# A long convolution by FFT ahead of a wave MLP: the setup written in another order, with the inverse's e tables made in the first inverse

## The chip, the cores and the metric

The kernel runs on one core of a Trainium2 chip. The metric is device time in microseconds (us) of one execution. The time before is the median of three runs, 2074.11 us (2072.76 to 2074.3). Besides, one execution was recorded by the hardware profiler, and all durations below come from it. Engines are called PE (matrix products; PEld is its weight load), DVE (VectorE), ACT (ScalarE), POOL (GpSimd) and SP (SyncE, which only issues DMAs here).

## The reference, cut to what matters

```python
# x (8, 5696, 128), h (5696, 128), all float32
L = 2 * S                                    # 11392
Yf = np.fft.rfft(x, n=L, axis=1) * np.fft.rfft(h, n=L, axis=0)[None]
x = np.fft.irfft(Yf, n=L, axis=1)[:, :S, :]  # the long convolution
theta = x @ w_theta
y = einsum('ts,bsd->btd', w_tok_r, x * cos(theta)) \
  + einsum('ts,bsd->btd', w_tok_i, x * sin(theta))
u = x + y
out = u + maximum(u @ w_ch, 0)
```

The change touches only the convolution, and of it the tables, h's transform and the first of eight groups of x.

## The kernel before, in words

**The transform.** The length 11392 is N1 x N2 = 178 x 64. Of the 178 frequencies of the first direction, K1 = 90 are kept (the rest follow by symmetry), and the sequence fills NB = 89 rows. A forward transform has two stages. *Stage A* (`stage_a`, L229) multiplies the 89 rows of the data by the table `f1_t` (L238): 16 chunks of four products, each chunk in one PSUM tile that ACT (L245) or DVE (L243) copies into the tile `a`, turned. With `both` set, chunks 1, 3, 6, 8, 11 and 13 go to DVE and ten to ACT. *f2* (`f2`, L248) multiplies `a` by the table `w_t2` (L256): 12 chunks, eleven with 32 products and the last with eight, then after the last chunk WARM = 12 products on table data whose results nobody reads (L262).

**h.** Two POOL DMAs bring h into `u_t` (L123). Four copies on DVE (`h_copy`, L289) turn it to f16 in `h16`, 16 of each half's 64 columns at a time. Its stage A follows, then f2; `h_chunk` (L307) evicts each chunk on ACT (L315) or DVE (L313) into a staging in the two halves of the tile `uv_t`, halves the first and the last frequency (L318), and issues two DMA stores on SP's queue (L320) to `hf_hbm`: 24 stores. They reorder the data, so each group reads it back from there.

**x.** There are eight groups, four pairs of batches by two halves of the channels. Each has a stage A and a *stage B* (`stage_b`, L356): f2's chunks are evicted by ACT to `xs` (L372), multiplied on DVE by the spectrum of h (`hs`, L374, the last chunk in two parts L379) and written to `uv_t`. The spectrum's chunks come back through SP's queue (L365) into four `hs` buffers, chunk c+4 loaded when chunk c has been multiplied. *Stage C* (`stage_c`, L385) is the first inverse step: 16 chunks of 16 products with the tables `r_u` and `r_v` (L395, L396), evicted with the sign table `sgn` into the tile `g` by DVE (L403) or, for four chunks, by two ACT operations (L400, L401). *Stage D* (`stage_d`, L406) is the last step, with the table `e_t` (L418), into the tile `yt`, which SP stores (L433). For each group g, stage C of g is woven with stage A of g+1 and the loads of group g+2; then stage B of g+1 is woven with stage D of g. The loads of x are pairs of POOL DMAs (L145), eight pairs a group; from group 2 on, each pair stands behind a small POOL copy that reads a piece of `g` (L143), so that it starts only once stage C has come so far. PSUM has four tiles for all these stages.

**The tables.** Each is a sine or cosine of a number of turns. POOL counts indices (iota, L170) and multiplies them by a column of the small tile `lane` (L178; `lane` is made in L156 to L161 by iotas and four POOL scalings). DVE takes the whole turns off (`within`, L184 and L185) and makes the absolute value (L192); ACT takes the sine (L189) and the cosine (L196). The tables are `f1_t`; `w_t2` in three parts (`w_angles` L216, then `w_rest` L222, which fills the other columns by two DVE operations, L225 and L227); `r_u`, `r_v` (`r_table`, L331); `sgn` (`s_table`, L350); and `e_t` in three parts (`e_table`, L342, 90x979 each). `signs` (L208) makes the column `sign` on DVE. `make_identity` (L57) makes a matrix on POOL that only the later part reads.

**What sets the order.** A scheduler orders the instructions of the rest, but from L151 to L462 (`ordered`) DVE, ACT and POOL keep the order in which the code is written. An instruction that waits there holds back all that is written behind it for its engine. The written order of before: h's loads, lane, the turns of f1 and w, loads of x group 0, the turns of r; then on DVE f1's angles, signs, w_angles(0), w_angles(1), w_rest(0), the first h copy, w_rest(1), and stage A of h with the other copies at chunks 1, 3 and 5, w_angles(2) at 6 and w_rest(2) at 12; then h's f2; then the turns of e and the loads of x group 1 on POOL; the two r tables, the s table and e table 0; stage A of x group 0 with e table 1 in its middle; stage B of group 0 with e table 2 in its middle.

**The rest.** After the eight groups the kernel multiplies the result by `w_theta`, takes sines and cosines (L479 to L501), and mixes the tokens with two 5696 x 5696 matrices (products L1097 and L1176, sums L1183, transposes of the weights L791), where most of the time lies.

Of the kernel before, what the change touches and what calls it, by code (L numbers as in the profile page):

```python
# [10 lines left out]
F32 = mybir.dt.float32  # L11
BF16 = mybir.dt.bfloat16
# [10 lines left out]
def kernel(  # L23
# [10 lines left out]
    nc = tc.nc  # L34
# [19 lines left out]

    const_pool = ctx.enter_context(tc.tile_pool(name="const", bufs=1))
    ident_bf = const_pool.tile([P, P], BF16)
    make_identity(nc, ident_bf)  # L57
    half_pi = const_pool.tile([P, 1], F32)
    nc.vector.memset(half_pi, HALF_PI)
    zero_b = const_pool.tile([P, 1], F32)  # L60
# [97 lines left out]
    nc.gpsimd.iota(lane[:, 1:2], pattern=[[0, 1]], base=0, channel_multiplier=1,  # L158
                   allow_small_or_imprecise_dtypes=True)
    for n, (col, per) in enumerate(((1, N1), (0, NF), (0, N2), (1, NF))):  # L160
        nc.gpsimd.tensor_scalar(lane[:, n + 2:n + 3], lane[:, col:col + 1], 1.0 / per, None, op0=mult)  # L161
    of_k1, of_n2, of_r, of_e = (lane[:, n:n + 1] for n in range(2, 6))

    def index(pattern, tag):

        n = 1
        for _, c in pattern:
            n *= c
        k = s1.tile([P, n], F32, tag=tag, name=tag)
        nc.gpsimd.iota(k, pattern=pattern, base=0, channel_multiplier=0, allow_small_or_imprecise_dtypes=True)  # L170
        return k

    def turns_of(k, base, of, m, tag=None):

        n = k.shape[1]
        t = (s1.tile([P, n], F32, tag=tag, name=tag) if tag else
             s2.tile([P, 11 * NB], F32, tag="turn", name="turn")[:, :n])[:m]
        nc.gpsimd.tensor_scalar(t, k[:m], float(base), of[:m], op0=add, op1=mult)  # L178
        return t
# [8 lines left out]
    def sine(out_, r, sign):  # L188
        nc.scalar.activation(out_, r, AF.Sin, bias=zero_b[:r.shape[0]], scale=-sign * TWO_PI)  # L189
# [6 lines left out]
        nc.scalar.activation(out_, k, AF.Sin, bias=half_pi[:k.shape[0]], scale=-TWO_PI)  # L196

    f1_t = fc.tile([P, 2 * K1], F16)
    t_f1 = turns_of(index([[1, K1]], "k_f1"), 0, of_k1, NB, "t_f1")
    H2 = N2 // 2  # L200
    k_w = index([[1, WK], [N1, H2]], "k_w")
    t_w = [turns_of(k_w, WK * c, of_n2, P) for c in range(3)]
    w_t2 = keep.tile([P, K1, 3 * N2], F16, tag="keep", name="w_t2")
    assert WB + BT + 3 * P * 2 <= K1 * 3 * N2
# [3 lines left out]
    def signs():  # L208
        t, k = s1.tile([P, 1], F32, tag="s_t", name="s_t"), s1.tile([P, 1], F32, tag="s_k", name="s_k")
        nc.vector.tensor_scalar(t, lane[:, 1:2], 0.5, None, op0=mult)  # L210
        nc.vector.tensor_scalar(k, t, MAGIC, None, op0=add)
        nc.vector.scalar_tensor_tensor(t, k, MAGIC, t, op0=ALU.subtract, op1=ALU.subtract)
        absolute(k, t)
        nc.vector.tensor_scalar(sign, k, -4.0, 1.0, op0=mult, op1=add)
# [11 lines left out]
        w_ = w_.rearrange("p k (c u n) -> p k c u n", c=3, u=2)  # L226
        nc.vector.tensor_scalar(w_[:, :, :, 1], w_[:, :, :, 0], sign, None, op0=mult)  # L227

    def stage_a(lhs, both=False):  # L229

        st = {}

        def chunk(q):
            if q == 0:
                st["a"] = fa.tile([P, 2 * K1, HD], F16, tag="a", name="a_")
            ps = psum()
            for i in range(4):
                nc.tensor.matmul(ps[:, i // 2, (i % 2) * 2 * K1:(i % 2 + 1) * 2 * K1], lhs(q + i), f1_t[:NB],  # L238
                                 start=True, stop=True)
            a_out = st["a"][:, :, q:q + 4].rearrange("p k (a q) -> p k a q", a=2)  # L240
            a_in = ps[:, :, :4 * K1].rearrange("p a (q k) -> p k a q", q=2)
            if both and q // 4 % 5 % 2:
                nc.vector.tensor_copy(a_out, a_in)  # L243
# [4 lines left out]
    def f2(a_st, c):  # L248

        c0, ck = CHK[c]  # L250
        ps = psum()
        for j in range(ck):
            for ri in range(2):
                for e in range(2):
                    rows = slice(64 * e, 64 * e + 64)
                    nc.tensor.matmul(ps[:, e, j * HD:(j + 1) * HD],  # L256
                                     w_t2[rows, c0 + j, N2 * (1 - ri):N2 * (3 - ri)],
                                     a_st["a"][rows, ri * K1 + c0 + j, :],
                                     start=(ri == 0), stop=(ri == 1))
        if c == NCK - 1:  # L260
            for n in range(WARM):
                nc.tensor.matmul(ps[:, n % 2, ck * HD:ck * HD + 384], w_t2[:, 2, :P],  # L262
                                 w_t2[:, 0:2, :].rearrange("p k n -> p (k n)"), start=True, stop=True)
        return ps[:, :, :ck * HD].rearrange("p e (k d) -> p e d k", k=ck)
# [8 lines left out]

    for f in load_x(0):
        f()
    nc.gpsimd.memset(uv_t[:, 2 * UVW:], 0.0)
    k_r = index([[0, 2], [1, N2]], "k_r")
    t_r = [turns_of(k_r, 0, of_r, P, f"t_r{n}") for n in range(2)]
    k_f = within(t_f1)
    absolute(k_f, t_f1)  # L280
    sine(f1_t[:NB, K1:], t_f1, -1)
    cosine(f1_t[:NB, :K1], k_f)
    signs()
    w_angles(0)
    w_angles(1)
    w_rest(0)

    def h_copy(d0):
        nc.vector.tensor_copy(h16[:NB, :, :, d0:d0 + 16],  # L289
                              u_t[:NB, :N2 * D].rearrange("p (n h d) -> p h n d", h=2, d=HD)[:, :, :, d0:d0 + 16])  # L290

    h_copy(0)
    w_rest(1)
    steps, a_h = stage_a(lambda q: h16[:NB].rearrange("p h n d -> p (h n) d")[:, :, q], True)
    for n, f in enumerate(steps):
        if n in (1, 3, 5):
            h_copy(8 * n + 8)
        if n == 6:
            w_angles(2)
        if n == 12:  # L300
            w_rest(2)
        f()

    hst = [t[:, :6 * D * CK].rearrange("p (c h d k) -> p c h d k", c=6, h=2, k=CK) for t in (u_t, v_t)]
    nc.gpsimd.memset(hst[(NCK - 1) // 6][:, (NCK - 1) % 6], 0.0)

    def h_chunk(c):  # L307
        c0, ck = CHK[c]
        ps = f2(a_h, c)
        h_ = hst[c // 6][:, c % 6]  # L310
        dst = h_[:, :, :, :ck]
        if c % 3 == 1:
            nc.vector.tensor_scalar(dst, ps, 16.0 / NF, None, op0=mult)  # L313
        else:
            nc.scalar.activation(dst, ps, AF.Copy, scale=16.0 / NF)  # L315
        for cc, j in ((0, 0), (NCK - 1, CHK[-1][1] - 1)):
            if c == cc:
                nc.vector.tensor_scalar(dst[:, :, :, j], dst[:, :, :, j], 0.5, None, op0=mult)  # L318
        for ri in range(2):
            nc.sync.dma_start(  # L320
                hf_hbm[:, c, :, ri, :].rearrange("h p n -> p h n"),
                h_[64 * ri:64 * ri + 64].rearrange("p h d k -> p h (d k)"))

    for c in range(NCK):
        h_chunk(c)
    r_u = fc.tile([P, P], F16)
    r_v = fc.tile([P, P], F16)
# [1 line left out]
    sgn = fc.tile([P, N2], F32)  # L329

    def r_table(n_, r_):  # L331
        t = t_r[n_]
        for q0 in range(2):
            for q1 in range(2):
                a_ = t[64 * q0:64 * q0 + 64, 64 * q1:64 * q1 + 64]
                nc.vector.tensor_scalar(a_, a_, 0.25 * (1 + n_ + q0 - q1), None, op0=add)
        k = within(t)
        sine(k, t, 1)
        nc.vector.tensor_scalar(r_[:, :N2 + EN], k[:, :N2 + EN], 0.125, None, op0=mult)
        nc.vector.tensor_scalar(r_[:, N2 + EN:], k[:, N2 + EN:], -0.125, None, op0=mult)  # L340

    def e_table(n):  # L342
        n0, t = 11 * n, t_e[n]
        k = within(t)
        absolute(k, t)
        t3, k3 = (z.rearrange("p (n m) -> p n m", m=NB) for z in (t, k))
        sine(e_t[:K1, n0:n0 + 11, 1, :], t3, -1)
        cosine(e_t[:K1, n0:n0 + 11, 0, :], k3)
# [89 lines left out]
    zz_n, ZB = [0], 3  # L438
    groups = [(bp, dh) for bp in range(B // 2) for dh in range(2)]

    def front(g, both=False):
# [4 lines left out]
        steps, a_st = stage_a(lambda q: x16[:NB, :, q], both)  # L446
        return (steps, *stage_b(a_st, dh))

    k_e = index([[1, 11], [N2, NB]], "k_e")
    t_e = [turns_of(k_e, 11 * n, of_e, K1) for n in range(3)]  # L450
    for f in load_x(1):
        f()
    r_table(0, r_u)
    r_table(1, r_v)
    s_table()
    e_table(0)
    a0, load0, b0 = front(0, True)
    for f in load0:
        f()
    woven(a0, [lambda: e_table(1)])  # L460
    woven(b0, [lambda: e_table(2)])
    ordered.close()  # L462
    setup.close()
    fg = pool("fft_g", 1, conv, side="right")
# [774 lines left out]
```

## Time and profile before

| what | value |
|---|---|
| median of three runs | 2074.11 us (2072.76 to 2074.3) |
| the profiled execution, its own time | 2068.87 us |
| its span in the trace | 2067.1 us |
| mean granted clock of PE over the span | 0.985 |
| busy share of the span: PE, DVE, POOL, ACT | 94%, 77%, 47%, 31% |
| first product on PE starts | 17.72 us |
| h's f2 starts | 32.49 us |
| stores of h's spectrum, first and last issue on SP | 35.41 and 54.78 us |
| first load of the spectrum issued | 55.44 us |
| first multiply of group 0 | 65.03 us |
| last multiply of group 0 | 85.0 us |
| last multiply of group 0 to first multiply of group 1 | 85.0 to 105.59 us |

The span runs from the first to the last instruction in the trace; the profiled execution's own time lies 1.77 us above it, and 5.24 us under the median of the runs. Starts are counted from the start of the span. The first 106 us hold all that the change touches; after it, from the second group on, one group follows the other every 37.5 to 40.4 us (first DVE eviction of stage C to the next group's), and the token mixing fills the rest.

### The profile page before, as it was taken

Reading aid. Unit: us, or ns where it says so; the run is one execution under the profiler, and the core shown is the slowest. Engines: PE = TensorE matmul, PEld = TensorE weight load, DVE = VectorE, ACT = ScalarE, POOL = GpSimd, SP = SyncE. Lnnn points to the kernel's source line nnn. Section 1 sums busy time; section 2 is a strip of 40 time slices with the busy share of each in tenths; the row PEclk is TensorE's granted clock in tenths of the full one; section 3 lists DMA queues with packets and bytes.
Section 4 is the critical chain, followed back from the end, with each engine's and each line's share of the span. In section 5 each row is a group of like instructions: output and inputs, shape, how many; then the busy total and the mean of one; then the engine's idle time right before and its main releaser. Section 6 shows DMA issues by size and latency. Waiting matters only on the chain.

```text
span 2067.1 us, 41585 instructions
## 1 busy us (share of the span) xinstructions
PE 1948.0 (94%) x15688; PEld 1080.5 (52%) x15865; DVE 1584.9 (77%) x2806; ACT 639.2 (31%) x971; POOL 964.7 (47%) x1764
## 2 busy tenths in 40 slices
PE   4788998889999999999999999999999999999998
PEld 3788888754444444444444444444444444444444
DVE  7787787877788888888877666877778677777767
ACT  4777777872323232333300000011111111111111
POOL 8232321266435363545475644454453535454450
PEclk9799999999999999999999999999999999999999
DMA  9799996999889898999999899788796979788793
GB/s 122 128 159 162 157 153 194 232 270 229 145 176 179 173 177 161 173 179 171 178 163 163 122 226 248 112 138 145 133 157 123 154 129 152 138 142 152 125 155 89
DMA packets 504489, 335.00 MB, mean 162 GB/s; under 512 B 184999, under 2 KB 457511, under 8 KB 503303
## 3 DMA queue, kind: packets, MB, share of 16 engines
q0 software_dynamic: 322208, 156.75, 59.7%
q1 hardware_dynamic: 176096, 164.05, 27.8%
q10 hardware_dynamic: 5984, 11.54, 1.6%
q8 instruction: 124, 2.03, 0.4%
q14 instruction: 77, 0.63, 0.1%
HBM read 377.11 MB, written 92.49 MB: 227 GB/s over the span
## 4 chain that ended last, share of the span: by engine, by line
PE 63%; DVE 5%; issue 2%; POOL 2%; DMA 1%; ACT 0%; DVEq 0%; POOLq 0%
PE m L1176 58%; PE m L1097 2%; DVE c L1183 2%; POOL ring L590 1%; DVE b L732 1%; PE v L878 1%; PE utp L871 1%; PE m L1180 1%; DMA ring<-in_moe_w_tok_i_dram 1%; DVE wt L791 1%; PE theta_ps L477 0%; PE tpz L819 0%; PE m L1063 0%; DMA ring<-in_moe_w_tok_r_dram 0%; POOL wl L838 0%
## 5 line engine op out<-in xcount | busy, mean ns | idle before, releaser
L590 POOL DMA_DIRECT2D ring<-in_moe_w_tok_i_dram x720 | 388.5, 545 | 659.9 <-DVE wt L791 579.0
L590 POOL DMA_DIRECT2D ring<-in_moe_w_tok_r_dram x720 | 387.2, 545 | 148.6 <-DVE wt L791 83.8
L791 DVE STREAM_TRANSPOSE wt<-ring 128x384 f32<-128x384 f32 (+2 forms) x720 | 360.0, 525 | 112.5 <-PE m L1176 69.3
L1176 PE MATMUL m<-b,wt 128*128 128x512 bf16 x1599 | 386.2, 380 | 4.1 <-DVE wt L791 1.7
L1176 PEld LDWEIGHTS <-wt 128*128 128x128 bf16 x1804 | 176.4, 98 | 219.8 <-DVE wt L791 7.5
L1183 DVE TENSOR_TENSOR c<-c,m 128x512 f32<-128x512 f32 x412 | 266.2, 672 | 0.4 <-PE m L1176 0.4
L873 ACT ACTIVATE ring<-utp 128x512 bf16<-128x512 bf16 x85 | 50.8, 597 | 582.5 <-PE utp L871 582.5
L395 PE MATMUL ps<-r_u,uv_t 128*128 128x128 f16 x1024 | 126.7, 220 | 9.0 <-DVE uv_t L379 5.9
L396 PE MATMUL ps<-r_v,uv_t 128*128 128x128 f16 x1024 | 125.8, 220 | 0.4
L374 DVE TENSOR_TENSOR uv_t<-xs,hs 128x2048 f16<-128x2048 f16 x88 | 105.9, 1225 | 25.6 <-ACT xs L372 15.5
L1097 PE MATMUL m<-b,wt 128*128 128x512 bf16 x466 | 111.2, 385 | 8.0 <-DMA b<-z_hbm 3.5
L868 ACT ACTIVATE ub<-c 128x512 bf16<-128x512 f32 x88 | 55.1, 629 | 191.0 <-DMA ring<-in_moe_w_tok_r_dram 112.4
L145 POOL DMA_DIRECT2D x<-in_x_dram x128 | 97.9, 770 | 34.9 <-PE ps L238 20.2
L395 PEld LDWEIGHTS <-uv_t 128*128 128x128 f16 x1024 | 100.6, 98 | 7.5 <-DVE uv_t L379 7.0
L396 PEld LDWEIGHTS <-uv_t 128*128 128x128 f16 x1024 | 100.5, 98 | 4.7 <-issue 3.0
L372 ACT ACTIVATE xs<-ps 128x1024 f16<-128x1024 f32 x96 | 91.4, 978 | 30.5 <-DVE uv_t L374 17.1
L1097 PEld LDWEIGHTS <-wt 128*128 128x128 bf16 x528 | 51.2, 99 | 67.0 <-issue 8.8
L256 PEld LDWEIGHTS <-w_t 64*128 64x128 f16 x3240 | 60.0, 101 | 27.1 <-issue 20.8
L479 ACT ACTIVATE red<-theta_ps,magic 128x512 f32<-128x512 f32 (+1 forms) x46 | 31.6, 688 | 135.6 <-PE theta_ps L477 109.6
L238 PE MATMUL ps<-f_t,x 89*128 89x180 f16 x512 | 59.7, 255 | 8.8 <-DVE a__784 L243 8.7
L821 ACT ACTIVATE ring<-tpz 128x512 bf16<-128x512 bf16 (+1 forms) x46 | 27.5, 597 | 130.8 <-PE tpz L819 114.9
L501 ACT ACTIVATE mag<-mag,half_pi 128x512 f32<-128x512 f32 (+1 forms) x90 | 65.1, 724 | 0.0
(2916 smaller groups left out, 3746.8 us busy)
## 6 DMA issues: line engine op xcount, KB each, us to landing
ring<-in_moe_w_tok_r_dram POOLq DMA_DIRECT2D x352, 96.0 KB, 4.5
ring<-in_moe_w_tok_i_dram POOLq DMA_DIRECT2D x352, 96.0 KB, 4.9
ring<-in_moe_w_tok_r_dram POOLq DMA_DIRECT2D x352, 80.0 KB, 4.5
ring<-in_moe_w_tok_i_dram POOLq DMA_DIRECT2D x352, 80.0 KB, 3.9
hs<-hf_hbm SPq DMA_DIRECT2D x192, 128.0 KB, 3.2
cp_hbm<-c SPq DMA_DIRECT2D x88, 256.0 KB, 2.5
c<-cp_hbm SPq DMA_DIRECT2D x88, 256.0 KB, 4.5
out_dram<-c SPq DMA_DIRECT2D x88, 256.0 KB, 4.3
```

The lines of the kernel that those rows point to most:

```text
L145: nc.gpsimd.dma_start(x16[p0:p1, e, n0:n0 + 16, :HD], bass.AP(tensor=src.tensor, offset=src.offset + (p0 * N2 + n0) * D + dh * HD, ap=[[N2 ...
L256: nc.tensor.matmul(ps[:, e, j * HD:(j + 1) * HD], w_t2[rows, c0 + j, N2 * (1 - ri):N2 * (3 - ri)], a_st["a"][rows, ri * K1 + c0 + j, :], s ...
L372: nc.scalar.activation(xs[:, :, :, :ck], ps, AF.Copy)
L374: nc.vector.tensor_tensor(uv[:, :, :, c0:c0 + ck], xs.rearrange("p e d k -> p e (d k)").unsqueeze(1).to_broadcast([P, 2, 2, HD * CK]), hv. ...
L395: nc.tensor.matmul(o, u_t[:, at:at + P], r_u, start=True, stop=False)
L396: nc.tensor.matmul(o, v_t[:, at:at + P], r_v, start=False, stop=True)
L501: nc.scalar.activation(mag, mag, AF.Sin, bias=half_pi[:m], scale=-TWO_PI)
L590: nc.gpsimd.dma_start(wb[32 * i:32 * i + 32, :ng, :nj * 64], bass.AP(tensor=a.tensor, offset=a.offset + row0 * S + p * H + i * QR + j0 * 6 ...
L791: nc.vector.transpose(wt.rearrange("p j t r -> p (j t r)").bitcast(F32).rearrange("p (j g t) -> p g j t", j=TJ, g=4)[:, :ng, :nj], wb[:, : ...
L1097: nc.tensor.matmul(ms[n // 2 * 2 + h], a[n][:, j, :, r], bts_of[p][jj][n % 2 * 2 + h][:, r, :], start=(n % 2 == 0 and jj == 0 and r == 0), ...
L1176: nc.tensor.matmul(ms[q], a[q][:, j, :, r], bts[jj][q][:, r, :], start=(jj == 0 and r == 0), stop=(jj == NJ - 1 and r == 1 and q not in left))
L1183: nc.vector.tensor_tensor(c, z, ms[q], op=op)
```

## The change

In the first 106 us, operations are moved, a few are exchanged between engines, and twelve products are dropped:

- **Opening.** The identity is made after the loads of x group 0 are issued. The four scalings of `lane` run on DVE. Both index lists (f1's and w's) are made before f1's turns, and `signs` comes ahead of f1's angles on DVE.
- **t_r.** The offset of the r turns, eight DVE additions on 64x64 blocks before, becomes part of the POOL operation that makes the turns, which is cut into eight 64x64 blocks for that (two 128x128 before).
- **h.** The first two copies of h come directly after w_angles(1), the other two at chunks 2 and 4. w_rest(0) moves from ahead of the first copy to chunk 7, w_angles(2) from chunk 6 to 9, w_rest(1) from behind the first copy to behind stage A, and w_rest(2) from chunk 12 to ahead of the fourth chunk of h's f2.
- **Evictions.** `stage_a` takes a list of the chunks that DVE evicts: 1, 3, 5, 8, 10, 13 for h, and 1, 3, 6, 8, 11, 13, as before, for x group 0.
- **The twelve unread products** after f2 stay out for h; the groups of x keep them.
- **r and s tables.** Angles and sines of both r tables come first; the scalings and `sgn` follow within stage A of x group 0, behind chunks 5, 8 and 10.
- **e tables.** All three leave the setup. The turns of e (one iota and three multiplications on POOL, ahead of the loads of group 1) go; instead each of the three tables is made whole within stage C of group 0, now with its own iota, in temporary space in the `yt` buffer, one pair of pieces for all three, so that they come one after another.

```diff
-    make_identity(nc, ident_bf)
...
-        nc.gpsimd.tensor_scalar(lane[:, n + 2:n + 3], lane[:, col:col + 1], 1.0 / per, None, op0=mult)
+        nc.vector.tensor_scalar(lane[:, n + 2:n + 3], lane[:, col:col + 1], 1.0 / per, None, op0=mult)
...
-    t_f1 = turns_of(index([[1, K1]], "k_f1"), 0, of_k1, NB, "t_f1")
-    k_w = index([[1, WK], [N1, H2]], "k_w")
+    k_f1, k_w = index([[1, K1]], "k_f1"), index([[1, WK], [N1, H2]], "k_w")
+    t_f1 = turns_of(k_f1, 0, of_k1, NB, "t_f1")
...
-            if both and q // 4 % 5 % 2:
+            if q // 4 in by_dve:
...
-        if c == NCK - 1:
+        if c == NCK - 1 and warm:
             for n in range(WARM):
...
     for f in load_x(0):
         f()
+    make_identity(nc, ident_bf)
     nc.gpsimd.memset(uv_t[:, 2 * UVW:], 0.0)
     k_r = index([[0, 2], [1, N2]], "k_r")
-    t_r = [turns_of(k_r, 0, of_r, P, f"t_r{n}") for n in range(2)]
+    t_r = []
+    for n in range(2):
+        t_r.append(s1.tile([P, P], F32, tag=f"t_r{n}", name=f"t_r{n}"))
+        for q0 in range(2):
+            for q1 in range(2):
+                rows, cols = slice(64 * q0, 64 * q0 + 64), slice(64 * q1, 64 * q1 + 64)
+                nc.gpsimd.tensor_scalar(t_r[n][rows, cols], k_r[rows, cols], of_r[rows], 0.25 * (1 + n + q0 - q1),
+                                        op0=mult, op1=add)
+    signs()
     k_f = within(t_f1)
...
-    signs()
     w_angles(0)
     w_angles(1)
-    w_rest(0)
...
     h_copy(0)
+    h_copy(16)
+    steps, a_h = stage_a(lambda q: h16[:NB].rearrange("p h n d -> p (h n) d")[:, :, q], (1, 3, 5, 8, 10, 13))
+    for n, f in enumerate(steps):
+        if n in (2, 4):
+            h_copy(8 * n + 16)
+        if n == 7:
+            w_rest(0)
+        if n == 9:
+            w_angles(2)
+        f()
     w_rest(1)
-    steps, a_h = stage_a(lambda q: h16[:NB].rearrange("p h n d -> p (h n) d")[:, :, q], True)
-    for n, f in enumerate(steps):
-        if n in (1, 3, 5):
-            h_copy(8 * n + 8)
-        if n == 6:
-            w_angles(2)
-        if n == 12:
-            w_rest(2)
-        f()
...
-        ps = f2(a_h, c)
+        ps = f2(a_h, c, False)
...
     for c in range(NCK):
+        if c == 3:
+            w_rest(2)
         h_chunk(c)
...
     def r_table(n_, r_):
...
-        k = within(t)
-        sine(k, t, 1)
-        nc.vector.tensor_scalar(r_[:, :N2 + EN], k[:, :N2 + EN], 0.125, None, op0=mult)
-        nc.vector.tensor_scalar(r_[:, N2 + EN:], k[:, N2 + EN:], -0.125, None, op0=mult)
-
-    def e_table(n):
-        n0, t = 11 * n, t_e[n]
-        k = within(t)
+        k = within(t_r[n_])
+        sine(k, t_r[n_], 1)
+        return lambda: (
+            nc.vector.tensor_scalar(r_[:, :N2 + EN], k[:, :N2 + EN], 0.125, None, op0=mult),
+            nc.vector.tensor_scalar(r_[:, N2 + EN:], k[:, N2 + EN:], -0.125, None, op0=mult))
+
+    def e_table(n, st):
+        n0 = 11 * n
+        if n == 0:
+            st["e"] = fg.tile([P, NB, N2], BF16, tag="yt", name="e_turns").rearrange("p m n -> p (m n)").bitcast(F32)
+        t, k = (st["e"][:K1, i * 11 * NB:(i + 1) * 11 * NB] for i in range(2))
+        nc.gpsimd.iota(k, pattern=[[1, 11], [N2, NB]], base=n0, channel_multiplier=0,
+                       allow_small_or_imprecise_dtypes=True)
+        nc.gpsimd.tensor_scalar(t, k, of_e[:K1], None, op0=mult)
+        nc.vector.tensor_scalar(k, t, MAGIC, None, op0=add)
+        nc.vector.scalar_tensor_tensor(t, k, MAGIC, t, op0=ALU.subtract, op1=ALU.subtract)
         absolute(k, t)
...
-    k_e = index([[1, 11], [N2, NB]], "k_e")
-    t_e = [turns_of(k_e, 11 * n, of_e, K1) for n in range(3)]
     for f in load_x(1):
         f()
-    r_table(0, r_u)
-    r_table(1, r_v)
-    s_table()
-    e_table(0)
-    a0, load0, b0 = front(0, True)
+    r_rest = [r_table(0, r_u), r_table(1, r_v), s_table]
+    a0, load0, b0 = front(0, (1, 3, 6, 8, 11, 13))
     for f in load0:
         f()
-    woven(a0, [lambda: e_table(1)])
-    woven(b0, [lambda: e_table(2)])
+    for n, f in enumerate(a0):
+        f()
+        if n in (5, 8, 10):
+            r_rest.pop(0)()
+    for f in b0:
+        f()
...
         c_ = stage_c(st, last)
+        if g == 0:
+            now = [lambda n=n: e_table(n, st) for n in range(3)]
         woven((c_, 0.06 if a_ else 0.0, 1.0), (a_, 0.0, 0.7), now, load_, (load_x(g + 2, st), 0.1, 1.02))
```

More of the change, by code (lines that the diff above doesn't have):

```diff
@@ L227, in w_rest, with stage_a @@
         nc.vector.tensor_scalar(w_[:, :, :, 1], w_[:, :, :, 0], sign, None, op0=mult)
-    def stage_a(lhs, both=False):
+    def stage_a(lhs, by_dve=()):
         st = {}
@@ L246, in stage_a, with f2 @@
         return [lambda q=q: chunk(q) for q in range(0, HD, 4)], st
-    def f2(a_st, c):
+    def f2(a_st, c, warm=True):
         c0, ck = CHK[c]
@@ L331, in r_table @@
     def r_table(n_, r_):
[L332 to L336, printed above, removed]
-        k = within(t)
-        sine(k, t, 1)
-        nc.vector.tensor_scalar(r_[:, :N2 + EN], k[:, :N2 + EN], 0.125, None, op0=mult)
-        nc.vector.tensor_scalar(r_[:, N2 + EN:], k[:, N2 + EN:], -0.125, None, op0=mult)
-    def e_table(n):
-        n0, t = 11 * n, t_e[n]
-        k = within(t)
+        k = within(t_r[n_])
[13 more added lines that the diff above has]
+        nc.vector.scalar_tensor_tensor(t, k, MAGIC, t, op0=ALU.subtract, op1=ALU.subtract)
         absolute(k, t)
@@ L439, with front @@
     groups = [(bp, dh) for bp in range(B // 2) for dh in range(2)]
-    def front(g, both=False):
+    def front(g, by_dve=()):
         if g >= len(groups):
@@ L445, in front @@
         x16 = x16s[g].rearrange("p b n d -> p (b n) d")
-        steps, a_st = stage_a(lambda q: x16[:NB, :, q], both)
+        steps, a_st = stage_a(lambda q: x16[:NB, :, q], by_dve)
         return (steps, *stage_b(a_st, dh))
-    k_e = index([[1, 11], [N2, NB]], "k_e")
-    t_e = [turns_of(k_e, 11 * n, of_e, K1) for n in range(3)]
     for f in load_x(1):
         f()
-    r_table(0, r_u)
-    r_table(1, r_v)
-    s_table()
-    e_table(0)
-    a0, load0, b0 = front(0, True)
+    r_rest = [r_table(0, r_u), r_table(1, r_v), s_table]
+    a0, load0, b0 = front(0, (1, 3, 6, 8, 11, 13))
     for f in load0:
         f()
-    woven(a0, [lambda: e_table(1)])
-    woven(b0, [lambda: e_table(2)])
+    for n, f in enumerate(a0):
[4 more added lines that the diff above has]
+        f()
     ordered.close()
```

## The prediction

> **What bounds the kernel now.** I read the span in 40 slices first, then cut the first 106 us where the work changes hands, then took each cut's waits and rows.
>
> ```profile
> PE   4788998889999999999999999999999999999998
> PEclk9799999999999999999999999999999999999999
> ```
>
> PE is the bound from the third slice on. Only in the first two (51.7 us each) does it stand, and in the second its granted clock falls; the diff acts exactly there. The cuts (us; busy us and count of PE, PEld, DVE, ACT, POOL; clock; DMA):
>
> ```profile
> 0.00:17.70 17.70, 0.00 (x0) 0.00 (x0) 11.99 (x21) 6.19 (x7) 15.79 (x30) 1.00 0.95 115
> 17.70:32.50 14.80, 10.54 (x66) 9.38 (x66) 13.60 (x16) 9.19 (x12) 14.41 (x17) 1.00 0.96 60
> 32.50:44.50 12.00, 10.72 (x383) 9.83 (x384) 5.25 (x6) 7.27 (x8) 10.63 (x16) 1.00 1.42 142
> 44.50:61.70 17.20, 8.43 (x56) 7.42 (x55) 13.32 (x31) 10.45 (x15) 1.58 (x2) 0.61 1.21 226
> 61.70:85.00 23.30, 13.77 (x384) 11.31 (x383) 16.24 (x16) 15.91 (x18) 4.68 (x8) 0.71 0.52 120
> 85.00:105.60 20.60, 20.12 (x379) 19.80 (x378) 14.57 (x14) 15.63 (x24) 11.17 (x21) 1.00 0.99 91
> ```
>
> They are: the opening; stage A of h; f2 of h; tables and stage A of x; f2 and multiplies of group 0; stage C of group 0. In the first two DVE is the fullest but for POOL's issues, in the fifth DVE and ACT alternate, in the last PE is at 20.12 of 20.60. What PE waits for up to 90 us:
>
> ```profile
> PE ps L238 <- DVE h L289: 17.7, 1, 17.7
> PE ps L238 <- DVE a__784 L243: 8.7, 2, 7.4
> PE ps L256 <- ACT xs L372: 6.8, 3, 5.9
> ```
>
> The first is DVE's first copy of h. The second is the fourth cut: the r tables, s table and e table 0 stand on DVE and ACT ahead of the evictions.
>
> **Opening.** DVE and SP rows of before (start, duration, engine, line):
>
> ```profile
> 5.38 1.08 DVE L184 TENSOR_SCALAR whole<-t_f 89x90 f32<-89x90 f32 x1 [4.46 <-POOL t_f L178]
> 15.17 0.44 DVE L225 TENSOR_SCALAR w_t<-w_t 128x960 f16<-128x960 f16 x1
> 15.71 1.31 DVE L227 TENSOR_SCALAR w_t<-w_t,sign 128x2880 f16<-128x2880 f16 x1
> 16.95 0.71 DVE L289 COPY h<-uv_t 89x2048 f16<-89x2048 f16 x1
> ```
>
> DVE idles 4.46 us for t_f. The four lane scalings (1.07 on POOL, about 0.15 each on DVE by the 128x1 rows at 7.65 and 7.82) and signs (1.5 us, from 7.65 to 9.14) now lie in that idle time, and the identity pair (0.21+0.29) leaves POOL's front. POOL has the lane iotas at about 2.9, k_f (0.22) and k_w (1.08) by 4.3, t_f by 4.7; DVE has scalings and signs by about 5.0, then 2.2 for the f1 angles: the w angles start near 7.2, not 9.14. They take 6.03 and end at 13.2. w_rest(0), 1.78 us, no longer stands ahead of the copy, which ends at 13.9. PE starts near **14.0** instead of 17.72: **-3.7**. (The copy needs both loads of h; they landed at 10.35 and 12.34, so about a microsecond is spare.)
>
> A rule of the Trainium skill speaks against this: "SBUF — State Buffer", section "Who interferes with whom", says that DVE in its two-port modes, or with two SBUF inputs, shares a port pair with GpSimd, and that the second comer waits until the first is done. The first row above, 1.08 us for 89x90 beside a POOL iota where a larger 128x128 one took 0.23 later, agrees with that. By the rule the scalings and signs, now beside iotas, could give back some 0.8 us (an estimate, 1.08 less 0.23) of the opening. The sum goes without it.
>
> **Stage A and f2 of h.** After PE's start DVE had 14.3 us of work by its rows (evictions, three copies, w_rest(1) and (2), angles(2)); now w_rest(2), 2.04, and one copy leave, w_rest(0), 1.78, comes: 13.3. ACT still stands for the angles of step 9. The stage cannot be under 13 and should not pass 16; I take 15.3, so f2 starts at 29.3 instead of 32.49: **-3.2**. The 12 dummy matmuls (2.12 us) are dropped: I count 0, because they run after f2's last product, while the stores below set the end. Their other use, the clock: the clock was 0.5 from 48.1 in spite of them. If the 64 products of x's stage A ran at half clock (150 against 79 ns, +4.5 us), that too lies under the stores. Without that cover it would cost 4.5.
>
> **The round trip of hf.** h's spectrum goes to HBM and comes back in the same DMA queue's order:
>
> ```profile
> 35.41 19.99 SPq L320 DMA_DIRECT2D hf_hbm<-uv_t  x24
> 55.44 68.77 SPq L365 DMA_DIRECT2D hs<-hf_hbm  x54
> 32.64 9.04 POOL L145 DMA_DIRECT2D x<-in_x_dram  x12
> ```
>
> In before the first multiply (65.03) waited for ACT, not for hs, which was there at 59.34. After, the tables in front are gone (e table 0 alone 6 us of DVE and ACT), stage A of x ends at about 46, and **hs becomes what is late next**. First store: 2.8 after f2's start, 32.1. The 24 took 20.0 us beside the x loads of group 1; these now start near 27.6, not 32.64 (k_e and t_e, 5.4 with gaps, and lanes, 1.1, leave POOL; t_r's offset costs eight 64x64 instead of two of 0.87: 0.2 to 0.87 each, taken 0.37 near the 0.35 of 89x90), so they overlap the stores less at the end. At the bare 0.64 each the stores need 15.4, at the old pace 20.0: last issue 47.5 to 52.1, taken 50.4, nearer the old pace as x loads still stand beside the first two thirds. Then hs is issued at 51.0 and there 3.9 later, as before: first multiply at **54.9** (51.5 to 56.2) for 65.03: **-10.1**. uv_t is the staging of those stores, so no multiply can come before.
>
> **Multiplies.** The 11 full ones run at 1.25, the last pair 0.7, and e table 0's first two DVE operations (1.85) fall among them: 16.1, so uv_t is done at 71.0. In before it was 85.0, since all of e table 2 stood between them (72.5 to 77.5) and the first ones were paced by half-clock f2. **-14.0**.
>
> **Stage C of group 0** has to take the rest of e table 0 and all of 1 and 2. One such table on DVE, and what DVE has there anyway:
>
> ```profile
> 72.53 0.66 DVE L184 TENSOR_SCALAR whole<-turn 90x979 f32<-90x979 f32 x1
> 73.22 1.17 DVE L185 SCALAR_TENSOR_TENSOR turn<-whole,turn 90x979 f32<-90x979 f32 x1
> 74.43 0.67 DVE L192 TENSOR_SCALAR whole<-turn 90x979 uint32<-90x979 uint32 x1
> L403 DVE TENSOR_TENSOR g__1359<-ps,sgn 90x1024 f16<-90x1024 f32 x12 | 14.6, 1219 | 5.6 <-PE ps L396 5.6
> ```
>
> DVE gets 0.67 + 2 x 2.5 = 5.7 beside 14.6: 20.3 of 20.6. ACT gets 3 x 2.2 = 6.6 beside 15.5: 22.1. POOL makes 2 x (1.1 iota + 1.36) = 4.9, between copies that wait for g. The tables share one tile, so they follow one another: POOL, DVE, ACT, then POOL again, 2.5 + 2.5 + 2.2 = 7.2 a trip, and on each engine the waiting instruction holds what is written behind it: on POOL the gated loads of group 2, on DVE the g evictions, on ACT the evictions of stage A; these free PSUM for PE. Bounds: 0 (all in PE's cover) to 3 x 7.2 = 21.6 (all exposed). ACT alone asks for about 1.5 over 20.6; I take +4.5: that plus about half of POOL's and DVE's parts of two trips in which a queue stands before its data (two of 1.5). This is the weakest number. Add 0.7 for a possible half-clock piece as f2 waits for hs (0 to 2.5, group 3's loss by such a window). Group 1's first multiply: 71.0 + 20.6 + 5.2 = 96.8 for 105.6: **-9** rounded. Everything after is bound by PE and shifts as it is.
>
> **Sum.** The profiled run took 2068.87, span 2067.1 and 1.77 outside; minus 9 gives 2060. It lies 5.24 under the median of the runs, 2074.11; the median should come to 2074.1 - 9 = **2065**.
>
> **Rivals.** About 0.2% (4 us) is what a measurement of this kernel can tell from no change.
>
> A, as above, 2061 to 2069.5: **0.58**.
>
> D, stage C swallows the tables (+1.5) and the stores go at nearly the bare pace (-3): -15, near 2059. For it: ACT and DVE have idle there; PE's wait must be longer than four PSUM tiles to count. Against: x loads beside the stores. **0.16**.
>
> B, the change does little of what it says: the round trip stays at the old pace or longer, and stage C loses 9 or more, so the gain ends within 4 us of 2074: **0.15**. For it: POOL has 11.17 busy in the last cut, so its part of a trip comes late.
>
> C, slower, one mechanism: the three table trips in stage C are exposed, since POOL's iota stands behind a copy waiting for g, DVE behind POOL, ACT behind DVE, and PE has no free PSUM. Price 21.6 against the 14.1 gained: +7.5, 2081.6. It decides once stage C grows by more than 14.1 (more than 18.2 for slower by 0.2%). For it: the strict order in three engines. Against: four PSUM tiles, and ACT's own evictions go on before its sine. **0.11**.
>
> A and D make faster 0.74, B same 0.15, C slower 0.11. Range 2058 (D's bounds) to 2072 (half of B); C lies outside.
>
> **What would show it.** Right: PE's first product near 14, f2 of h near 29.3, first store 32, last 50.4, first multiply near 55 waiting for the DMA of hs, uv_t done near 71, stage C about 25 with DVE and ACT waiting for e_turns, later group periods unchanged at 37.5 to 40.4. Wrong: a first multiply over 58, stage C over 30, later groups longer, or a first copy that waits for h's DMA.

## The result, and the profile after

The changed kernel takes 2067.91 us (median of 17 runs, 2061.31 to 2073.08), the kernel before 2074.15 in the same comparison (17 runs, 2069.7 to 2079.86): ratio 0.9972, 95% interval 0.9963 to 0.9981, so 4 to 8 us less. The forecast was 2065 in 2058 to 2072, 9 us less. The profiled execution took 2061.31, the lowest of its runs, with a span of 2059.5; that of before (2068.87) lies below all 17 of its own. The profile of one experiment, e_early, was taken in a run slowed by a lower clock (2315.88 us at 0.842), so only its other times are used.

The cuts of the changed kernel at the same changes of work (columns as before):

```profile
0.00:13.90 13.90, 0.00 (x0) 0.00 (x0) 9.96 (x23) 5.80 (x7) 12.31 (x21) 1.00 1.18 130
13.90:29.00 15.10, 10.35 (x66) 9.54 (x67) 12.38 (x16) 9.52 (x13) 14.63 (x24) 1.00 1.18 74
29.00:41.00 12.00, 8.79 (x368) 8.29 (x368) 6.98 (x8) 7.11 (x8) 10.77 (x15) 0.94 1.43 140
41.00:56.30 15.30, 13.88 (x248) 13.46 (x247) 7.08 (x18) 9.79 (x14) 7.55 (x8) 0.50 1.31 235
56.30:73.80 17.50, 10.19 (x203) 7.21 (x197) 15.37 (x16) 11.81 (x13) 1.90 (x4) 0.70 0.72 182
73.80:102.70 28.90, 23.39 (x395) 22.30 (x393) 19.57 (x20) 20.54 (x29) 22.80 (x27) 0.94 0.76 65
```

The opening, the fourth cut and the fifth are shorter (13.9, 15.3 and 17.5 us for 17.7, 17.2 and 23.3), the second and third much as they were, and the last, stage C of group 0, takes 28.9 us for 20.6. Four of the waits up to 110 us in the changed kernel (engine, line, what for; total, times, longest):

```profile
PE ps L237 <- DVE h L295: 13.9, 1, 13.9
DVE uv_t L386 <- DMA hs<-hf_hbm: 9.3, 5, 6.2
DVE e_turns L355 <- POOL e_turns L354: 5.5, 2, 3.7
PE ps L407 <- DVE g__1319 L415: 3.0, 2, 1.8
```

The first copy comes at 13.9 (17.7 before). The second line is the new bound of the middle: DVE's first multiply waits 6.2 us for the spectrum's way through HBM. The third and fourth are the price of the e tables in stage C: DVE stands for POOL's turns, and PE for the g evictions behind them. SP's stores of h's spectrum in the changed kernel, merged:

```profile
31.96 20.22 SPq L327 DMA_DIRECT2D hf_hbm<-uv_t  x24
```

They start 3.45 us earlier and take as long as before. The times of the landmarks, from the timelines (us):

| kernel | first product | f2 of h | first multiply | last multiply ends | group 1's first multiply | from there to the end |
|---|---|---|---|---|---|---|
| before | 17.72 | 32.49 | 65.03 | 85.01 | 105.59 | 1961.5 |
| changed | 13.91 | 28.99 | 56.29 | 73.84 | 102.72 | 1956.8 |
| e_none | 13.90 | 29.01 | 58.35 | 77.29 | 100.43 | 1959.5 |
| e_gap | 13.88 | 28.96 | 60.71 | 82.22 | 102.82 | 1963.8 |
| e_setup | 13.86 | 28.95 | 58.00 | 80.75 | 101.35 | 1963.8 |
| e_stagec | 17.73 | 31.95 | 61.42 | 80.13 | 111.60 | 1961.7 |
| e_none2 | 13.89 | 28.97 | 57.54 | 76.25 | 99.61 | 1956.5 |
| e_twoop | 13.88 | 28.96 | 57.61 | 75.14 | 100.79 | 1963.7 |
| x1_late | 13.86 | 28.94 | 57.62 | 79.33 | 103.20 | 1965.8 |
| before_2 | 17.68 | 32.44 | 69.81 | 91.49 | 112.09 | 1965.2 |
| after_2 | 13.89 | 28.98 | 56.85 | 74.32 | 103.28 | 1962.4 |
| warm_h | 13.88 | 28.98 | 57.07 | 74.95 | 106.47 | 1965.2 |
| e_twoop_2 | 13.88 | 28.98 | 58.26 | 75.99 | 102.74 | 1958.6 |

So the first pair of profiles differs by 7.6 us, of which only 2.9 lie in the part that the change touches. The last column scatters over 9 us whatever the edit; a difference there in one pair of profiles says nothing.

### The profile page after: what moved, and what is told of

Same layout as the page of the kernel before. It is cut to its first block, busy times and chain, and to the rows that moved or that the text cites. A ratio compares the mean times of both kernels' runs of the same rounds, so it can differ in the third digit from the quotient of the medians.

```text
span 2059.5 us, 41560 instructions
## 1 busy us (share of the span) xinstructions
PE 1948.4 (95%) x15676; PEld 1080.2 (52%) x15853; DVE 1580.0 (77%) x2802; ACT 639.7 (31%) x971; POOL 977.6 (47%) x1768
## 4 chain that ended last, share of the span: by engine, by line
PE 60%; DVE 5%; DMA 4%; POOL 2%; issue 2%; ACT 0%; DVEq 0%; POOLq 0%
PE m L1189 56%; DMA ring<-in_moe_w_tok_r_dram 2%; POOL ring L601 2%; DVE c L1196 2%; DMA ring<-in_moe_w_tok_i_dram 1%; PE v L891 1%; PE utp L884 1%; DVE wt L804 1%; PE m L1193 1%; DVE b L745 1%; PE theta_ps L488 0%; PE tpz L832 0%; DMA wl<-in_moe_w_tok_i_dram 0%; PE m L1076 0%; PE m L1110 0%
## 5 line engine op out<-in xcount | busy, mean ns | idle before, releaser
L804 DVE STREAM_TRANSPOSE wt<-ring 128x384 f32<-128x384 f32 (+2 forms) x720 | 358.9, 523 | 111.6 <-PE m L1189 69.8
L386 DVE TENSOR_TENSOR uv_t<-xs,hs 128x2048 f16<-128x2048 f16 x88 | 105.5, 1223 | 25.7 <-DMA hs<-hf_hbm 14.8
L384 ACT ACTIVATE xs<-ps 128x1024 f16<-128x1024 f32 x96 | 91.8, 977 | 34.6 <-DVE uv_t L386 23.1
L745 DVE TENSOR_TENSOR b<-b 128x1024 bf16<-128x1024 bf16 x100 | 61.4, 680 | 0.0
```

The costliest lines, as they stand in the source:

```text
L384: nc.scalar.activation(xs[:, :, :, :ck], ps, AF.Copy)
L386: nc.vector.tensor_tensor(uv[:, :, :, c0:c0 + ck], xs.rearrange("p e d k -> p e (d k)").unsqueeze(1).to_broadcast([P, 2, 2, HD * CK]), hv. ...
L745: return [lambda f=f, x=x: f(*x) for f, x in ((nc.vector.tensor_sub, (bt[M3], b12, b22)), (nc.vector.tensor_sub, (bt[M4], b21, b11)), (nc. ...
L804: nc.vector.transpose(wt.rearrange("p j t r -> p (j t r)").bitcast(F32).rearrange("p (j g t) -> p g j t", j=TJ, g=4)[:, :ng, :nj], wb[:, : ...
```

## The experiments

Theory T: the gain comes from the earlier first copy; the middle is then set by the round trip of h's spectrum; and stage C gives most of it back, because the e tables are made there in a fixed order on three engines. Rival H: stage C is long by the half clock at its start and the loads of group 2. Rival M: the moved tables carry the gain. Ratios are to the kernel before, run beside each set of experiments; behind each ratio stands its 95% interval.

**e_none and e_none2: no e tables.** `e_t` is only set to 0, on POOL in the first and on DVE in the second.

```diff
-            now = [lambda n=n: e_table(n, st) for n in range(3)]
# e_none, behind load_x(1):
+    nc.gpsimd.memset(e_t, 0.0)
# e_none2, ahead of stage B:
+    nc.vector.memset(e_t, 0.0)
```

> Leaves out the making of the e tables altogether (e_t is set to 0 on POOL, so the output is not the reference's). Theory T (the table trips, in order on three engines, cost most of what stage C of group 0 gained in length): first multiply stays at 56 us, the last one comes at about 72 (two DVE operations less), stage C takes 22.3 (20.6 of the kernel before plus 1.7 of half clock), group 1's first multiply near 94.3 instead of 102.7, median 8 us under the changed kernel's, near 2060. Rival H (stage C is long because of the half clock and the loads of group 2): stage C stays over 27 and the median within 2 us of the changed kernel's.

> As e_none, the changed kernel without the e tables (the output is not the reference's), but e_t is set to 0 on DVE while it waits for hs, since the POOL operation that set it there ran beside a DVE one of the r tables that took 5.96 us and held up stage A. Theory T: first multiply 56.3, last near 72.5, stage C 22.5, group 1's first multiply near 95, 7.7 us before the changed kernel's 102.7. Rival H: stage C over 27.

Measured: e_none ratio 0.9938 (0.9922 to 0.9955), stage C 23.1; e_none2 0.9954 (0.9941 to 0.9966), stage C 23.4. Without the tables stage C is 5.5 us shorter than in the changed kernel (28.9), and only 2.8 over the 20.6 of before: T holds and H explains the smaller part. By the ratios the medians lie 7 and 4 us under the changed kernel's, where 8 was expected. Stage C of e_none2:

```profile
76.30:99.60 23.30, 22.97 (x383) 22.71 (x384) 14.64 (x12) 15.62 (x24) 11.13 (x21) 0.88 0.85 73
```

The granted clock, third from the end of such a line, splits the stage further (an estimate: where PE sets the pace, the length times one less the clock is what the half clock took). In before, before_2, e_setup and e_gap the clock over stage C is 1.00, and the stage takes 20.6. Here it is 0.88, which is 2.8 us: all that the stage is longer. In the changed kernel it is 0.94, 1.7 us, so the tables took the other 6.6 of the 8.3, more than the plain difference of 5.5 says.

Group 1's first multiply came at 99.6 in e_none2, not at 95, mostly because the multiplies took 18.7, not 16. In e_none the write on POOL did harm of its own. Rows of DVE, then of POOL:

```profile
40.22 0.33 DVE L183 TENSOR_SCALAR whole<-t_r 128x128 f32<-128x128 f32 x1
40.79 5.96 DVE L183 TENSOR_SCALAR whole<-t_r 128x128 f32<-128x128 f32 x1
```

```profile
41.65 5.01 POOL L448 MEMSET e_t<- 128x5874 f16 x1
```

The same DVE operation took 0.33 us, then 5.96, and ended as POOL's write of 5.01 us did; in the twelve other profiles read here the second one takes 0.22 to 0.34. The Trainium skill's page "SBUF — State Buffer", section "Who interferes with whom", says that when DVE in a two-port mode and GpSimd want the shared port pair, the one that issues second is blocked outright and not slowed. The rows agree in that DVE stood until the write was done. But by these rows DVE began 0.86 us before the write, so they do not show that it was the second.

**e_setup: the change without the moved tables.** r, s and e tables go back to their old places. The opening, the new t_r, the order of h's part and the dropped twelve products stay.

```diff
-            now = [lambda n=n: e_table(n, st) for n in range(3)]
+    k_e = index([[1, 11], [N2, NB]], "k_e")          # ahead of load_x(1), as before
+    t_e = [turns_of(k_e, 11 * n, of_e, K1) for n in range(3)]
+    for f in r_rest:                                 # ahead of stage A
+        f()
+    e_table(0)
+    woven(a0, [lambda: e_table(1)])
+    woven(b0, [lambda: e_table(2)])
```

> The changed kernel with the r, s and e tables at the places that they had before: only the new opening, the order of h's part and the dropped dummy products remain. Theory T: everything comes 3.5 us earlier than in the kernel before: first product 13.9, first multiply 61.5, last 81.5, group 1's first multiply 102, median 3.5 under before, near 2070.5, so as good as the whole change within 3 us. Rival M (moving the tables carries the gain): group 1's first multiply near 105, no gain.

Measured: 2067.15, ratio 0.9966 (0.9952 to 0.9979), stage C 20.6, group 1's first multiply at 101.35. So these parts together are worth as much as the whole change; no run takes the opening apart from the rest of them, and warm_h below tries only the twelve products. The ratio is 7 us under before, twice what T gave, and the first multiply came at 58.0, not 61.5: 7.0 us earlier than in before, though the first product is only 3.9 earlier. It waits for the spectrum here too (3.8 us).

**e_stagec: the moved tables alone,** put into the kernel before (its e_table replaced by the new one, the turns dropped from the setup).

> The kernel before with only the e tables moved into stage C of group 0 (their turns on POOL with them). Theory T: first product still 17.7, first multiply near 59.5 since it now waits for hs, last near 77, stage C near 29, group 1's first multiply near 106: no gain, within 2 us of before. Rival M: group 1's first multiply near 102.5 and 3 us under before.

Measured: 2075.07, ratio 1.0000 (0.9987 to 1.0013); first multiply 61.42 for 65.03, but stage C 31.5, so group 1 starts at 111.6. No gain, as T had it, though group 1 starts 5.6 us later than expected: stage C was 2.5 longer, with a clock of 0.86 over it (4.4 us by the same estimate, which leaves 6.5 for the tables), the multiplies took 18.7, and the first of them came 1.9 late. M falls.

**e_gap: the tables where the spectrum is awaited.** Turns on POOL behind the loads of group 1, tables 0 and 1 ahead of stage B, table 2 in its middle.

```diff
+    e_table(0)
+    e_table(1)
+    woven(b0, [lambda: e_table(2)])
```

> The changed kernel with the e tables back in the setup, but where DVE and ACT stand idle for hs: turns on POOL behind the loads of group 1, tables 0 and 1 between stage A and the first multiply of group 0, table 2 among the multiplies. Theory T: first multiply at 56 to 58, last at 74 to 76, stage C 22.5, group 1's first multiply at 97 to 98, median about 5 us under the changed kernel's, near 2063. Rival H: stage C stays over 27, no gain.

Measured: 2069.65, ratio 0.9982 (0.9971 to 0.9993): no gain over the changed kernel, and by the medians 2 us worse, though the intervals overlap. T's 5 us did not come, and H falls too: stage C is 20.6. But the first multiply comes at 60.71, 4.4 later than in the changed kernel, and the multiplies take 21.5, 4.0 longer; that is all that stage C gained. ACT shows why the first one is late:

```profile
54.33 1.11 ACT L188 ACTIVATE e_t<-turn,zero_b 90x979 f16<-90x979 f32 x1 [3.98 <-DVE turn L184]
55.82 1.13 ACT L195 ACTIVATE e_t<-whole,half_pi 90x979 f16<-90x979 f32 x1 [0.37 <-DVE whole L191]
57.65 1.11 ACT L188 ACTIVATE e_t<-turn,zero_b 90x979 f16<-90x979 f32 x1 [0.71 <-DVE turn L184]
58.67 1.11 ACT L195 ACTIVATE e_t<-whole,half_pi 90x979 f16<-90x979 f32 x1
59.68 1.91 ACT L377 ACTIVATE xs<-ps 128x1024 f16<-128x1024 f32 x2
```

The sines stand ahead of the xs evictions, waiting for DVE, and the xs come at 59.68 instead of 52.37.

**e_early: the tables under the stores.** Turns ahead of the loads of group 1, tables 0 and 1 ahead of chunks 6 and 10 of h's f2, table 2 behind the first two xs evictions.

```diff
+        if c in (6, 10):
+            e_table(c // 4 - 1)
         h_chunk(c)
...
+    pres[0](0)                  # f2 and xs eviction of chunks 0 and 1 alone
+    pres[0](1)
+    e_table(2)
```

> The changed kernel with the e tables where DVE and ACT have idle time by its trace: turns on POOL ahead of the loads of group 1, table 0 ahead of chunk 6 and table 1 ahead of chunk 10 of h's f2 (the stores are behind the evictions there), table 2 behind stage A of x after the first two xs evictions, while hs is awaited. Theory T (tables cost only what is not under the round trip of hf): first multiply 56 to 58, last 73 to 75, stage C 21 to 23, group 1's first multiply near 96.5, median 6 under the changed kernel's. Rival (DVE and ACT are full wherever tables go): no gain over the changed kernel, as in e_gap.

Measured: 2064.1, ratio 0.9953 (0.994 to 0.9965), some 4 us under the changed kernel by the ratios, with intervals that just overlap. That is nearer to T's 6 than to the rival's 0; the landmarks could not be read.

**e_twoop and e_twoop_2: another form for the turns.** The rows of the changed kernel had shown POOL's multiplication of e's turns at twice the price taken for it. In the kernel before the same step adds a number and multiplies in one instruction; the changed kernel only multiplies.

```diff
-        nc.gpsimd.tensor_scalar(t, k, of_e[:K1], None, op0=mult)
+        nc.gpsimd.tensor_scalar(t, k, 0.0, of_e[:K1], op0=add, op1=mult)
```

> The changed kernel with the turns of e made by the two-operation form (add 0, then multiply) that the kernel before used and that took 1.12 to 1.62 us there, against 2.75 for the one-operation form in the changed kernel. If the form sets the time, each of the three falls to 1.1 to 1.6 and stage C gets 1.5 to 3 us shorter, group 1's first multiply near 100.5, median 2 under the changed kernel's. If the place sets it (source and target in one tile, or work beside it), it stays at 2.75 and nothing changes.

> e_twoop once more beside after_2, since it is the candidate for a version that beats both. If the two-operation form is worth what the trace said, group 1's first multiply is near 100.8, 2 us before after_2's, and the median 2 us under after_2's; if that was chance, both agree within 1 us.

The second table's turns on POOL, in the changed kernel and then in e_twoop:

```profile
80.50 2.75 POOL L354 TENSOR_SCALAR e_turns<-e_turns,lane 90x979 f32<-90x979 f32 x1
```

```profile
81.89 1.09 POOL L354 TENSOR_SCALAR e_turns<-e_turns,lane 90x979 f32<-90x979 f32 x1
```

Only the form differs, so the form sets the time. Stage C of e_twoop_2:

```profile
76.00:102.70 26.70, 24.36 (x392) 23.50 (x390) 19.53 (x19) 20.51 (x29) 19.41 (x27) 0.88 0.81 67
```

Stage C takes 25.7 and 26.7 us (28.9 and 29.0 in the two profiles of the changed kernel). The clock over it was 0.93 and 0.88, so by the same estimate the tables cost 3.2 and 2.9 us there instead of 6.6. DVE's wait for the turns falls from 5.4 (after_2) to 2.0 (e_twoop_2), and PE's waits for g evictions there fall from 3.0 (after_2) to 0.2 (e_twoop_2). Times: 2062.87, ratio 0.9956 (0.9943 to 0.9968), and 2063.87, ratio 0.9951 (0.9936 to 0.9966), beside after_2's 2067.51, ratio 0.9971 (0.9959 to 0.9982): measured side by side 3.6 us less. This version beats both kernels, the one before clearly, the changed one by both medians, with intervals that just overlap.

**x1_late: are the stores slowed by the loads of x?**

```diff
-    for f in load_x(1):
+    for f in load_x(1, {"g": last_h.rearrange("p h d k -> p h (d k)")}):
         f()
```

> The changed kernel with the loads of x group 1 held back until h's last chunk is staged (each pair behind a small POOL copy that reads it), so that they start near 41 instead of 29 us and the first stores have the DMAs to themselves. If the loads slow the stores (the prediction's reason for its 18.3 us), the stores run at 0.64 us each until 41, the last is issued near 47 to 49, and the first multiply comes at 53 to 54; group 1's first multiply 2 us earlier. If SP or the stores themselves set the pace, the last stays at 51.6 and nothing changes.

Measured: the loads start at 40.6; the first twelve stores are issued within 9.3 us (31.55 to 40.88), 0.85 apart, where the changed kernel needed 10.3 (31.96 to 42.26), 0.94 apart. But the last is issued at 50.69 for 51.57, the first multiply is at 57.62, and group 1's at 103.2. The 0.09 between the two paces is not the loads' doing: in after_2, with the loads beside them, the first twelve take 9.2 us (31.93 to 41.14). From first to last issue the 24 stores took 19.1 us here and 17.8 to 20.0 in the twelve other profiles read here, so the second alternative holds: SP or the stores themselves set the pace, and the prediction's reason for its 18.3 falls. The landmarks behind the first multiply do not compare, since tables 0 and 1 came among the multiplies in this kernel (these took 21.7, and stage C only 23.9). Ratio 0.9956 (0.9943 to 0.9969): the median is lower than the changed kernel's, while the landmarks show no gain; its profile was its slowest run (2070.78), so this stays open.

**warm_h: the twelve unread products kept.**

```diff
-        ps = f2(a_h, c, False)
+        ps = f2(a_h, c)
```

> The changed kernel with the twelve unread products after h's f2 kept. Prediction: they cost nothing, since hs is awaited until 56 us: first multiply within 0.7 us of after_2's, group 1's first multiply too. Rival: they hold the clock at full speed over stage A of x (half speed in the changed kernel from 40 us), so stage A ends some 4 us earlier, with no gain before hs comes, but with a full clock at the start of stage C, worth 1.7 us.

Measured: 2069.94, ratio 0.9985 (0.9972 to 0.9998), 2.4 us over after_2, with intervals that overlap; first multiply 57.07 for 56.85, group 1's at 106.47 for 103.28. Half of the rival came: the clock over stage A of x is nearly full (0.89 from 41 to 56 us, against 0.66 in after_2). Stage C of group 0, in warm_h and then in after_2:

```profile
75.00:106.50 31.50, 25.87 (x397) 24.96 (x396) 19.60 (x20) 20.80 (x29) 22.82 (x27) 0.86 0.69 58
```

```profile
74.30:103.30 29.00, 23.50 (x397) 22.42 (x395) 19.57 (x21) 20.83 (x30) 22.83 (x27) 0.94 0.75 63
```

DVE, ACT and POOL have the same work; PE works 2.4 us more at a lower clock. By the same estimate the half clock took 4.4 us here and 1.7 in after_2, and the tables 6.5 and 6.6: the stage is longer by the clock alone. So in this profile the clock was up where nobody waited for PE, and down later, where PE is the bound. e_stagec, which also keeps the products, shows the same 31.5 and 0.86. Whether that is a rule or where the clock's pieces happened to fall, two profiles do not settle; and this profile (2073.52) is among the slower of its runs.

**before_2 and after_2: a second profile of each.**

> The kernel before once more, for a second profile. If the 4.7 us by which the rest of the span (from group 1's first multiply to the end) was longer before (1961.5) than after (1956.8) came from the change, it is 1961 to 1962 here again; if it is chance of the clock's windows and of instruction fetches, it may lie anywhere from 1956 to 1966, as in the experiments so far, while group 1's first multiply stays at 105 to 106.

> The changed kernel once more, on the chip of the others of this call. By chance alone: group 1's first multiply at 102 to 103.5, the rest anywhere from 1956 to 1966. By a cause in the change: the rest near 1957 again. Median 3 to 7 under the kernel before.

The rest of the span was 1965.2 and 1962.4. This pair differs by 2.8 the same way, but both lie in the 1956.5 to 1965.8 that the variants cover, so no cause in the change is shown for the 4.7 us. But before_2's landmark was not at 105 to 106: it was 112.09, the run took 2079.11. PE's rows from the last products of h's f2 on, in before and then in before_2:

```profile
40.58 1.24 PE L256 MATMUL ps<-a__184,w_t 64*128 64x64 f16 x73 [1.28 <-issue]
41.74 2.12 PE L262 MATMUL ps<-w_t 128*128 128x384 f16 x12
```

```profile
42.76 2.13 PE L256 MATMUL ps<-a__184,w_t 64*128 64x64 f16 x73 [4.07 <-issue]
44.82 4.02 PE L262 MATMUL ps<-w_t 128*128 128x384 f16 x12
```

PE stands 4.07 us, not 1.28, for nothing that the profile names; then the clock is half, and the last products and the twelve unread ones take 2.8 us longer. Nearly all of it reaches the first multiply (69.81 for 65.03): in both profiles that one waits for ACT's xs behind PE (3.53 us), not for the spectrum. The changed kernel has such a stop too:

```profile
38.36 1.24 PE L255 MATMUL ps<-a__187,w_t 64*128 64x64 f16 x73 [2.05 <-issue]
```

There it costs nothing that the landmarks show, since hs is not there before 56 us: with a stop of 2.05 the first multiply was at 56.29, with 0.98 (after_2) at 56.85, with 3.47 (e_none2) at 57.54, and with 0.99 (e_twoop_2) at 58.26. x1_late has a stop of 1.57 with no x load in flight, so the x loads alone do not make it.

The traces hold a likely cause. The stop comes at the same place every time, ahead of the last 73 products of f2. In all twelve profiles that have it (0.71 to 4.07 us; e_setup has none, e_early is left aside), PE goes on 1.2 to 1.6 us after a 16 KB packet has ended on the DMA queue that the profile calls instruction (q8). That packet ends at 39.30 us in before and at 41.26 in before_2, and PE goes on at 40.58 and 42.76. So PE most likely waited for its own instructions. No run moved that packet, and why it came late is open.

## Why the prediction was right, and where not

The direction and the range held; the size was 9 for 5.8. The chain of causes was right: an earlier opening, the spectrum's round trip as the new bound, and tables that give part of it back in stage C. But three terms were too favourable, and that the median still fell into the range is in part luck (see the sum).

- **Opening:** right. Predicted 14.0 and -3.7, measured 13.91 and -3.8. The scalings and signs ran in the idle time at 3.18 to 4.33, beside POOL's iota (3.25 to 4.37), and the estimate from the port rule (0.8 us back) did not come: signs were shorter there than before (0.9 for 1.5).
- **Stage A of h:** right, 15.1 for 15.3.
- **Round trip:** the right bound, its terms too small. The stores took 19.6 from first to last issue, not 18.3; the first multiply came at 56.3 and 56.9, not 54.9. No run shows the lower end of 15.4: even with no x load in flight the stores went 0.85 apart. That the loads slow them, the reason given for 18.3, is not shown by any run; the loads also began at 29.2, not 27.6.
- **Multiplies:** 17.5, not 16.1 (its own terms add up to 16.3), since hs is late for later chunks too (behind the first wait of 6.2 us three more, 2.1 together). Together with the round trip, -11.2 for -14.0.
- **Stage C:** +8.3, not +5.2. Both terms were too small. The tables took 6.6, not 4.5, and the mis-sized part is POOL's in a trip: 1.36 us was taken from the two-operation rows of before, and the one-operation form took 2.75. With the old form the tables cost 2.9 and 3.2, and the stage is 5.1 and 6.1 longer, near the forecast. The half clock at its start took 1.7, not 0.7, and up to 4.4 in other profiles.
- **The twelve products at nothing:** not shown right. Keeping them cost 2.4 us by the medians, with intervals that overlap; in the one profile the loss lies not under the stores but in stage C's clock.
- **Sum:** group 1's first multiply was 2.9 earlier in the first pair of profiles, not 9: the terms above took 2.8 (round trip and multiplies) and 3.1 (stage C) from it. That the median moved by 6 is not that pair's difference of 7.6, 4.7 of which lies behind the landmark; in the second pair the landmark differs by 8.8 (112.09 and 103.28). Carrying one profile's difference over to the median is a step that the runs do not bear out. The forecast also did not price that the new order hides a stop of PE, which made the first multiply 4.8 later in before_2 than in before. But before's own stop of 1.28 lies in the middle of the twelve, so how much of the 5.8 such stops are, two pairs do not tell. That the terms fell short by 6 and the median still came out in the range is luck as far as these profiles show.
- **Rivals:** C's mechanism, exposed trips, was there, but cost 6.6 of the 21.6; that four PSUM tiles and ACT's own evictions cover the rest is argued, not tried. D failed on both of its conditions. B's came nearest: the stores kept the old pace (19.6 for 19.4), stage C lost 8.3 of its 9, and the first pair's landmark gained only 2.9. That the median moved by 6 all the same, outside of B, these profiles do not account for.

## What to carry to other kernels

Make a moved operation pay for its place by reading what stands behind it on every engine: tables that share one buffer and hop POOL, DVE, ACT cost a PE-bound stage 6.6 us here, while with the same tables in the setup (e_setup) the whole took no longer. Price an instruction by the same form, not only by the same shape. And profile both kernels twice before explaining a difference of 0.3%: the parts that no edit touches moved by 9 us.

## What was not expected of the hardware

- POOL's 90x979 multiplication took 2.75 us with one operation and 1.09 with an added 0 as the first of two, in three instances of each in the changed kernel and e_twoop.
- A DVE 128x128 operation took 5.96 us beside a 5.01 us POOL write, 0.33 just before.
- PE stopped for up to 4.1 us at one place within h's f2, in twelve profiles, and went on 1.2 to 1.6 us after a 16 KB packet of the instruction queue had ended; in before_2 the half clock that followed doubled the next products' time (2.12 to 4.02 us for the same twelve).
